# Two decode layers of cached attention and a gated feed-forward block: kept keys scored through PSUM in pairs of tiles, the last pairs' scores by unit, softmax sums inverted per head, the last column blocks in two PSUM tiles

## The chip, the cores and the metric

The kernel runs on one core of a Trainium2 chip. The metric is the device time of one execution in microseconds (us). Before the change the median of three runs is 1321.85 us (1321.67 to 1322.05).

## The reference

The reference runs two identical layers on two sequences (B = 2) with one new token each. All data are 32-bit floats. The weights and the caches are the same in both layers.

```python
B, Sq, D = 2, 1, 448
H, Sk, Dh = 16, 4096, 256          # feed-forward width F = 1792

def _A_ref(x, k_cache, v_cache, wq, wo):
    q = transpose((x @ wq).reshape(B, Sq, H, Dh), 0, 2, 1, 3)
    scores = einsum("bhqd,bhkd->bhqk", q, k_cache) * (Dh ** -0.5)
    p = softmax(scores)
    o = einsum("bhqk,bhkd->bhqd", p, v_cache)
    return transpose(o, 0, 2, 1, 3).reshape(B, Sq, H * Dh) @ wo

def _B_ref(x, W_gate, W_up, W_down):
    gate, up = x @ W_gate, x @ W_up
    return ((gate * (gate > 0)) * up) @ W_down

x = A_x
for _ in range(2):
    x = x + _A_ref(layernorm(x), A_k_cache, A_v_cache, A_wq, A_wo)
    x = x + _B_ref(layernorm(x), B_W_gate, B_W_up, B_W_down)
```

Keys and values of all heads and sequences are 268 MB, and each layer reads nearly all of them: the page counts 562.56 MB read.

## The kernel before

**Units and chunks.** A unit is one head of one sequence, so a layer has 32 units, numbered u in the order in which the layer treats them; the units 2j and 2j+1 are the two sequences of one head. The 4096 keys of a unit lie as 32 tiles of 128 partitions x 256 elements (`NT`), in four chunks (`NC`) of eight tiles (`CT`). A chunk is 1 MB, and so are the slots of `arena`, the one large SBUF buffer: 3 x 8 + 3 = 27 slots. The second layer treats the units in another order that begins with the last units of the first.

**Loads.** All loads are issued by SyncE (SP) from one list in a fixed order. `pump` issues the next loads while there are free slots, and `release` puts a slot back and pumps again. A load into a slot therefore waits for the last reader of the slot. 20 chunks (`KEPT`) at the end of the first layer stay in the arena for the second layer, and one value chunk more: the keys of the first layer's units 29, 30 and 31 (12 chunks) and the values of units 30 and 31, with one chunk of 29. The feed-forward weights follow: seven loads "in" (gate and up) and four loads "out". In the first layer the loads in0 to in4 find slots before the feed-forward block begins; in5 takes the slot of in0, which is free when TensorE has used in0, and what follows takes slots in the same way.

**Scores.** VectorE (DVE) multiplies a unit's keys with its query, and the products are summed over the 256 elements of a tile by VectorE or by ScalarE (ACT). Most units go through `score_block`: two products of 128x4096 in place (L378), eight tiles summed by ACT (L383), the rest by one reduction (L387). Units whose keys come in single chunks go through `score`:

- Kept keys must not be overwritten. Each tile is one scalar_tensor_tensor instruction (L419), which multiplies and sums at once; its product goes to `junk`, a part of the tile `down` that nobody reads. It has 8 such instructions per chunk.
- The last two units of the second layer (`CLOSING`) take four of a chunk's eight tiles by one product of 128x1024 (L410) and ACT (L412), the other four by L419 in place.
- Other chunks of the first units of the second layer share the eight tiles between L410 with ACT and L419 or L416 in other proportions.

**The loop over the units** is written out by hand in `attention`, and each engine keeps that order. Step u scores unit u chunk by chunk (c = 0 to 3), and between the chunks it finishes unit u-2: `out_add` (DVE, L475), `out_turn` (TensorE, L483), `out_keep` (DVE, L494), and `project` (TensorE, L504) if u-2 is odd. Then come `softmax_sum` of unit u-1 (L447) and the last chunk's scores; then the maximum (L428), the sum across the partitions by POOL, the exponentials (ACT, L438); then `weigh` of unit u-1, the product of its probabilities with its values (TensorE, L459), and `out_copy` of u-1 (ACT, L472). So TensorE does not weigh unit u-1 before `out_keep` of unit u-2, when that is odd, has run on VectorE in the middle of the scores of unit u.

**The division by the softmax sum** is in `out_turn`: the matmul that turns the row of results into a column is taken with `ri`, the inverted sum, as its moving operand.

**The feed-forward block** (`ffn`) multiplies with in0 to in6 (L569), turns the hidden values (L639), and multiplies with the four loads out0 to out3, one block of output columns each (`block`, L662). At the end of the kernel the four blocks go by turns into the two halves of one PSUM tile, `po_all`, and ACT copies each block out (L688). `busy` issues matmuls that nobody reads (L244).

Of the kernel before, what the change touches and what calls it, by code (L numbers as in the profile page):

```python
# [29 lines left out]
HASTE = 5  # L30
# [39 lines left out]
def two_layers(  # L70
# [9 lines left out]
    nc = tc.nc  # L80
# [58 lines left out]
    def get(*key):  # L139
        at = at_of[key]  # L140
        return arena[:, at * UNIT : (at + 1) * UNIT]

    def release(*key):
        units.free.add(at_of.pop(key))
        pump()
# [48 lines left out]

    row = consts.tile([P, 2 * DH], F32, name="row")
    down = consts.tile([P, D], F32, name="down")
    junk = down[:, :DH]
    y_end_row = row[SUMS : SUMS + B, D:]
    nc.scalar.dma_start(row[:B, :D], x.rearrange("b s d -> (b s) d"))
    pump()  # L200
# [4 lines left out]
    ones = consts.tile([P, 1], F32, name="ones")  # L205
# [26 lines left out]
    po_all = ps_o.tile([P, 2, 2 * DH], F32, name="po")  # L232
# [7 lines left out]
    def busy(n):  # L240


        unread = ps_q.tile([P, n * TAIL], F32, name="pq")
        nc.tensor.matmul(  # L244
            unread[:B], ident[:, :B], ident[:, None, :TAIL].to_broadcast([P, n, TAIL]),
            start=True, stop=True,
        )
# [46 lines left out]
    def attention(order, after, q_first=None, begun=None):  # L294
# [5 lines left out]
        q_of, oT_of, s_of, mx_of, p_of, r_of, po_of, pT_of = ({} for _ in range(8))  # L300
# [68 lines left out]
        def score_block(u, c):  # L369


            at = at_of["k", order[u], 0] * UNIT
            kt = arena[:, at : at + NC * UNIT].rearrange("p (t n) -> p t n", t=NT)
            if c == 0:
                s_of[u] = work.tile([P, NT], F32, name="scores")
            if c % 2 == 0:
                some = kt[:, c * CT : (c + 2) * CT, :]
                nc.vector.tensor_mul(  # L378
                    some, some, q_of[u][:, None, :].to_broadcast([P, 2 * CT, DH])
                )  # L380
            if c == 0:
                for t in range(CT):
                    nc.scalar.activation(  # L383
                        kt[:, t, :], kt[:, t, :], AF.Copy, accum_out=s_of[u][:, t : t + 1]
                    )
            if c == NC - 1:
                nc.vector.reduce_sum(s_of[u][:, CT:], kt[:, CT:, :], axis=AX.X)  # L387
                blocks.remove(("k", order[u]))
                for k in range(NC):
                    release("k", order[u], k)  # L390

        def score(u, c):
            kept = ("k", order[u], c) in after
            if ("k", order[u]) in blocks and not kept and not (ahead and u < HASTE):
                return score_block(u, c)
            kt = get("k", order[u], c).rearrange("p (t n) -> p t n", t=CT)
            if c == 0:
                s_of[u] = work.tile([P, NT], F32, name="scores")
            found = s_of[u][:, c * CT : (c + 1) * CT]
            by_act = 0 if kept else BY_ACT  # L400
            whole = CT
            if ahead and (u < HASTE or u >= n_u - CLOSING):
                by_act = CT // 2 if u > 0 else BY_ACT if c > 0 else 0
                whole = by_act
            whole = whole if by_act else 0
            if by_act:


                some = kt[:, :whole, :]
                nc.vector.tensor_mul(some, some, q_of[u][:, None, :].to_broadcast([P, whole, DH]))  # L410
                for t in range(by_act):
                    nc.scalar.activation(  # L412
                        kt[:, t, :], kt[:, t, :], AF.Copy, accum_out=found[:, t : t + 1]
                    )
            if whole > by_act:
                nc.vector.reduce_sum(found[:, by_act:], kt[:, by_act:, :], axis=AX.X)  # L416
            else:
                for t in range(whole, CT):
                    nc.vector.scalar_tensor_tensor(  # L419
                        junk if kept else kt[:, t, :], kt[:, t, :], 1.0, q_of[u],  # L420
                        op0=ALU.mult, op1=ALU.mult, accum_out=found[:, t : t + 1],
                    )
            if not kept:
                release("k", order[u], c)
# [7 lines left out]
        def softmax_exp(u):  # L432
            b = order[u][1]
            nm = work.tile([P, 1], F32, name="nm")
            nc.scalar.activation(nm, mx_of.pop(u), AF.Copy, scale=nsr[:, b : b + 1])  # L435
            p_of[u] = work.tile([P, NT], F32, name="probs")
            rs = work.tile([P, 1], F32, name="rs")
            nc.scalar.activation(  # L438
                p_of[u], s_of.pop(u), AF.Exp, bias=nm, scale=sr[:, b : b + 1], accum_out=rs
            )  # L440
            r_of[u] = work.tile([P, 1], F32, name="total")
            nc.gpsimd.partition_all_reduce(r_of[u], rs, P, RED.add)  # L442

        def softmax_sum(u):
            total = r_of[u]
            r_of[u] = work.tile([P, 1], F32, name="ri")
            nc.vector.reciprocal(r_of[u], total)  # L447

        def weigh(u, c):

# [27 lines left out]
            )  # L478

        def out_turn(u):  # L480
            pT_of[u] = ps_s.tile([P, 2], F32, name="small")
            for c in range(2):
                nc.tensor.matmul(  # L483
                    pT_of[u][:, c : c + 1], row[:, c * P : (c + 1) * P], r_of[u],
                    start=True, stop=True,
                )
            if u == n_u - 1:
                busy(2)

        def out_keep(u):  # L490
            h, b = order[u]
            if h not in oT_of:
                oT_of[h] = work.tile([P, 2, B], F32, name="oT")
            nc.vector.tensor_copy(oT_of[h][:, :, b], pT_of.pop(u))  # L494

        def project(u):
            h = order[u][0]
# [22 lines left out]
        for u in range(n_u + 2):  # L520
# [19 lines left out]
            if ahead and u == 0:  # L540
                query(ahead)
            if_pair(softmax_sum, u - 1)
            if mixed:
                if_pair(weigh, u - 1, 2)
# [8 lines left out]
    def ffn(last):  # L553
# [4 lines left out]
        total = squares()  # L558
        if not last:
            h, b = second[0]  # L560
# [107 lines left out]
        if last:  # L668


            square = work.tile([P, B], F32, name="square")
            nc.vector.tensor_mul(square, rstd, rstd)
            close = work.tile([P, CLOSE, B], F32, name="close")
            for i, st in enumerate(stat[-CLOSE:]):
                nc.vector.tensor_mul(
                    close[:, i, :], square, st.rearrange("p (b r) -> p b r", b=B)[:, :, 0]
                )
            y_end = ps_f.tile([P, TAIL], F32, name="pf")[SUMS : SUMS + B]
            nc.tensor.matmul(y_end, unit, y_end_row, start=True, stop=False)
            pds = [po_all[:, c % 2, :D] for c in range(FULL + 1)]  # L680

            def to_y(at, stop):
                nc.tensor.matmul(y[:, at], scaled, down[:, at], start=False, stop=stop)

            for c in range(FULL):
                at = block(pds[c], c, range(14))
                release("out", "", c)
                nc.scalar.activation(down[:, at], pds[c][:, at], AF.Copy)  # L688
                if c > 0:
                    to_y(before, False)  # L690
                before = at
            at = block(pds[FULL], FULL, range(14 - CLOSE))
            nc.scalar.activation(down[:, at], pds[FULL][:, at], AF.Copy)
            to_y(before, True)
            nc.vector.tensor_copy(left, y_left)
            nc.sync.dma_start(found[:, : FULL * P], left)
            w = get("out", "", FULL)
            for i in range(CLOSE):
                k = 14 - CLOSE + i
                w_k = w[:, k * TAIL : (k + 1) * TAIL]  # L700
# [24 lines left out]
        total = work.tile([P, 1], F32, name="sums")  # L725
# [39 lines left out]
    found = out.rearrange("b s d -> (b s) d")  # L765
# [62 lines left out]
```

## Time and profile before

| what | value |
|---|---|
| median of three runs | 1321.85 us |
| the profiled execution | 1322.23 us, of which its span is 1320.3 us |
| TensorE matmuls busy | 579.8 us (44%) |
| VectorE busy | 994.1 us (75%) |
| ScalarE busy | 330.1 us (25%) |
| GpSimd busy | 101.6 us (8%) |
| read from memory | 562.56 MB, 426 GB/s over the span |

The profiled execution took 1.93 us more than its span, and 0.38 us more than the median. In the profile, times are microseconds from the span's start. A row of the timeline has the start, the duration, the engine, the line, the operation, its output and inputs, and the count of instructions merged in the row; in brackets stands the idle time before it and what ended that. A row of a group has the count, the busy time, the mean duration in ns, and the idle time before them.

### The profile page before, as it was taken

What the parts mean: (1) busy time and instruction counts of PE and PEld (TensorE: products, weight loads), DVE (VectorE), ACT (ScalarE), POOL (GpSimd) and SP (SyncE); (2) the same over time, 40 slices, a digit from 0 to 9 for tenths busy, and PEclk for the clock granted to TensorE, in tenths of its full rate; (3) what the DMA queues carried; (4) which work ended last, traced back from release to release, by engine and by line L of the source; (5) the groups of instructions that cost most, each with busy time, mean ns of one, the idle gap of its engine ahead of it and who ended that gap; (6) DMA issues with size and microseconds to landing.
All of it is one profiled execution on the core that took longest, in us unless ns stands there. A gap on an engine that the chain in (4) does not pass through costs nothing.

```text
span 1320.3 us, 10001 instructions
## 1 busy us (share of the span) xinstructions
PE 579.8 (44%) x3276; PEld 193.0 (15%) x3276; DVE 994.1 (75%) x953; ACT 330.1 (25%) x1416; POOL 101.6 (8%) x192
## 2 busy tenths in 40 slices
PE   3333354333443334434585454352443424534358
PEld 2111111111111111111141111110111101111113
DVE  4878787787777877788729987688786887877971
ACT  2212222122221222221026522122122221222251
POOL 0000000000000000010001131000000000000110
PEclk9665666656666667667697767656766656666579
DMA  9999999999999999999999999999999999999998
GB/s 407 435 439 429 423 429 441 428 437 431 424 440 430 437 433 425 433 427 430 420 385 415 430 431 438 433 429 435 433 432 433 431 429 437 433 425 430 429 421 334
DMA packets 22671, 563.21 MB, mean 427 GB/s; under 512 B 2520, under 2 KB 2652, under 8 KB 9564
## 3 DMA queue, kind: packets, MB, share of 16 engines
q1 hardware_dynamic: 22612, 562.57, 99.4%
q8 instruction: 26, 0.43, 0.1%
q14 instruction: 25, 0.20, 0.0%
q10 hardware_dynamic: 8, 0.00, 0.0%
HBM read 562.56 MB, written 0.00 MB: 426 GB/s over the span
## 4 chain that ended last, share of the span: by engine, by line
DMA 62%; DVE 25%; PE 8%; issue 1%; ACT 1%; POOL 1%; SPq 0%; DVEq 0%; POOLq 0%; ACTq 0%
DMA arena<-in_vk_dram 61%; DVE arena L378 13%; DVE scores L387 7%; PE po L459 2%; DVE arena L410 2%; DVE arena L419 2%; PE pq L337 1%; DMA arena<-in_w_in_dram 1%; PE acc L504 1%; POOL top L430 1%; DVE down L419 1%; DVE row L475 1%; PE pf L569 1%; PE po L662 1%; ACT arena L412 1%
## 5 line engine op out<-in xcount | busy, mean ns | idle before, releaser
L378 DVE TENSOR_TENSOR arena<-arena 128x4096 f32<-128x4096 f32 x102 | 450.8, 4420 | 215.8 <-DMA arena<-in_vk_dram 215.8
L387 DVE TENSOR_REDUCE scores<-arena 128x24 f32<-128x6144 f32 x53 | 346.2, 6533 | 0.0
L459 PE MATMUL po<-arena,probs 128*2 128x512 f32 x2048 | 313.1, 760 | 21.2 <-DMA arena<-in_vk_dram 12.9
L483 PE MATMUL small<-ri,row 128*128 128x1 f32 x256 | 61.6, 344 | 574.1 <-DVE row L475 574.1
L383 ACT ACTIVATE arena<-arena 128x256 f32<-128x256 f32 x424 | 170.2, 403 | 330.7 <-DVE arena L378 330.7
L483 PEld LDWEIGHTS small<-ri,row 128*128 128x128 f32 x256 | 56.1, 306 | 635.0 <-DVE row L475 635.0
L435 ACT ACTIVATE nm<-top,nsr 128x1 f32<-128x1 f32 x64 | 18.8, 294 | 361.5 <-POOL top L430 361.5
L504 PE MATMUL acc<-arena,oT 128*2 128x448 f32 x128 | 50.9, 893 | 109.0 <-DVE oT L494 109.0
L430 POOL PARTITION_ALL_REDUCE top<-mx x64 | 44.5, 695 | 628.5 <-DVE mx L428 628.5
L459 PEld LDWEIGHTS po<-arena,probs 128*2 128x2 f32 x2048 | 53.8, 98 | 228.0 <-issue 216.9
L337 PE MATMUL pq<-arena,xs 128*33 128x256 f32 x174 | 76.1, 605 | 12.6 <-DMA arena<-in_w_head_dram 12.6
L383 ACT ACTIVATION_READ_ACCUMULATOR arena<-arena 128x1 f32 x424 | 79.4, 187 | 0.0
L353 POOL PARTITION_BROADCAST arena<-arena x58 | 27.7, 547 | 479.1 <-ACT arena L349 479.1
L349 ACT ACTIVATE arena<-pq 33x256 f32<-33x256 f32 x29 | 10.9, 377 | 174.0 <-PE pq L341 174.0
L475 DVE SCALAR_TENSOR_TENSOR row<-po,lead,row 128x256 f32<-128x256 f32 x64 | 30.6, 479 | 29.6 <-ACT row L472 29.3
L412 ACT ACTIVATE arena<-arena 128x256 f32<-128x256 f32 x117 | 47.1, 404 | 15.4 <-DVE arena L410 15.0
L472 ACT ACTIVATE row<-po,lead 128x256 f32<-128x256 f32 x64 | 29.6, 462 | 45.5 <-PE po L459 45.5
L337 PEld LDWEIGHTS pq<-arena,xs 128*33 128x33 f32 x174 | 25.4, 163 | 80.1 <-issue 66.1
L410 DVE TENSOR_TENSOR arena<-arena 128x1024 f32<-128x1024 f32 (+1 forms) x24 | 33.4, 1392 | 1.9 <-DMA arena<-in_vk_dram 1.9
L442 POOL PARTITION_ALL_REDUCE total<-rs x64 | 28.8, 450 | 61.7 <-ACT probs L438 60.6
L419 DVE SCALAR_TENSOR_TENSOR down<-arena,pq 128x256 f32<-128x256 f32 x64 | 26.9, 420 | 6.2 <-DMA arena<-in_vk_dram 4.2
L419 DVE SCALAR_TENSOR_TENSOR arena<-arena 128x256 f32<-128x256 f32 x80 | 29.1, 418 | 0.0
(142 smaller groups left out, 365.8 us busy)
## 6 DMA issues: line engine op xcount, KB each, us to landing
arena<-in_vk_dram SPq DMA_DIRECT2D x16, 4096.0 KB, 40.1
arena<-in_w_head_dram SPq DMA_DIRECT2D x31, 896.0 KB, 32.0
arena<-in_vk_dram SPq DMA_DIRECT2D x27, 1024.0 KB, 14.6
arena<-in_vk_dram SPq DMA_DIRECT2D x12, 2048.0 KB, 38.8
arena<-in_w_in_dram SPq DMA_DIRECT2D x14, 896.0 KB, 27.1
arena<-in_w_out_dram SPq DMA_DIRECT2D x5, 896.0 KB, 8.9
arena<-in_vk_dram SPq DMA_DIRECT2D x47, 44.3
arena<-in_w_out_dram SPq DMA_DIRECT2D x1, 512.0 KB, 16.4
```

The lines of the kernel that those rows point to most:

```text
L337: nc.tensor.matmul(q, xs[:, c, :], w[:, c * DH : (c + 1) * DH], start=(c == 0), stop=False)
L378: nc.vector.tensor_mul(some, some, q_of[u][:, None, :].to_broadcast([P, 2 * CT, DH]))
L383: nc.scalar.activation(kt[:, t, :], kt[:, t, :], AF.Copy, accum_out=s_of[u][:, t : t + 1])
L387: nc.vector.reduce_sum(s_of[u][:, CT:], kt[:, CT:, :], axis=AX.X)
L410: nc.vector.tensor_mul(some, some, q_of[u][:, None, :].to_broadcast([P, whole, DH]))
L412: nc.scalar.activation(kt[:, t, :], kt[:, t, :], AF.Copy, accum_out=found[:, t : t + 1])
L419: nc.vector.scalar_tensor_tensor(junk if kept else kt[:, t, :], kt[:, t, :], 1.0, q_of[u], op0=ALU.mult, op1=ALU.mult, accum_out=found[:, ...
L430: nc.gpsimd.partition_all_reduce(mx_of[u], mx, P, RED.max)
L459: nc.tensor.matmul(po_of[u][32 * t : 32 * t + 2, :], p_of[u][:, n : n + 2], vt[:, 2 * t * DH : (2 * t + 2) * DH], start=(c == 0), stop=(c ...
L475: nc.vector.scalar_tensor_tensor(row[:, :DH], po_of.pop(u)[:, DH:], lead[:, 1:2], row[:, :DH], op0=ALU.mult, op1=ALU.add,)
L483: nc.tensor.matmul(pT_of[u][:, c : c + 1], row[:, c * P : (c + 1) * P], r_of[u], start=True, stop=True,)
L504: nc.tensor.matmul(acc[at : at + B], oT_of[h][:, c, :], wo[:, c * D : (c + 1) * D], start=(n < 3), stop=(n >= n_u - 3),)
```

## The change

Four edits:

1. A kept chunk is scored in four steps of two tiles. Each step is a product of 128x512 into a PSUM tile (`pf`, pool `ps_f`, two buffers) and a reduction of it to 128x2. `junk` is gone.
2. The last two units of the second layer take all eight tiles by one product of 128x2048; ACT sums four of them as before, and one reduction on VectorE sums the other four.
3. The two softmax sums of a head stand in one tile and are inverted by one instruction after the second unit. `out_turn` multiplies with ones, and `out_keep` runs once per head and multiplies both units' columns with the inverted sums.
4. At the end of the kernel the four column blocks go by turns into `po_all` and into a second PSUM tile from `ps_f`.

```diff
-    junk = down[:, :DH]
@@ score
             whole = CT
             if ahead and (u < HASTE or u >= n_u - CLOSING):
                 by_act = CT // 2 if u > 0 else BY_ACT if c > 0 else 0
-                whole = by_act
+                whole = by_act if u < HASTE else CT
             whole = whole if by_act else 0
...
-            if whole > by_act:
+            if kept:
+                for t in range(0, CT, 2):
+                    some = ps_f.tile([P, 2, DH], F32, name="pf")
+                    nc.vector.tensor_mul(
+                        some, kt[:, t : t + 2, :], q_of[u][:, None, :].to_broadcast([P, 2, DH])
+                    )
+                    nc.vector.reduce_sum(found[:, t : t + 2], some, axis=AX.X)
+            elif whole > by_act:
                 nc.vector.reduce_sum(found[:, by_act:], kt[:, by_act:, :], axis=AX.X)
             else:
                 for t in range(whole, CT):
                     nc.vector.scalar_tensor_tensor(
-                        junk if kept else kt[:, t, :], kt[:, t, :], 1.0, q_of[u],
+                        kt[:, t, :], kt[:, t, :], 1.0, q_of[u],
@@ softmax_exp, softmax_sum
-            r_of[u] = work.tile([P, 1], F32, name="total")
-            nc.gpsimd.partition_all_reduce(r_of[u], rs, P, RED.add)
+            if u % 2 == 0:
+                r_of[u] = work.tile([P, B], F32, name="total")
+            total = r_of[u - u % 2]
+            nc.gpsimd.partition_all_reduce(total[:, b : b + 1], rs, P, RED.add)
...
-            r_of[u] = work.tile([P, 1], F32, name="ri")
-            nc.vector.reciprocal(r_of[u], total)
+            if u % 2 == 0:
+                return
+            total = r_of[u - 1]
+            r_of[u - 1] = work.tile([P, B], F32, name="ri")
+            nc.vector.reciprocal(r_of[u - 1], total)
@@ out_turn, out_keep
-                    pT_of[u][:, c : c + 1], row[:, c * P : (c + 1) * P], r_of[u],
+                    pT_of[u - u % 2][:, c, b : b + 1], row[:, c * P : (c + 1) * P], ones,
...
-            nc.vector.tensor_copy(oT_of[h][:, :, b], pT_of.pop(u))
+            share = r_of.pop(u - 1)[:, None, :].to_broadcast([P, 2, B])
+            nc.vector.tensor_mul(oT_of[h], pT_of.pop(u - 1), share)
@@ ffn
-            pds = [po_all[:, c % 2, :D] for c in range(FULL + 1)]
+            pds = [po_all[:, 0, :D], ps_f.tile([P, D], F32, name="pf")] * 2
```

On VectorE, the beginning of the scores of the first layer's unit 30, a kept unit, stood before as follows (`mx` is the maximum of unit 29, `pq` the PSUM tile with the query, `row` that of `out_add`):

```order
228 L428 TENSOR_REDUCE mx<-scores 128x1 [waits DVE_49]
229 L419 SCALAR_TENSOR_TENSOR down,scores<-arena,pq 128x256 [waits DMAHW1_49,PE_49]
230 L419 SCALAR_TENSOR_TENSOR down,scores<-arena,pq 128x256 [waits DVE_49] x7
231 L475 SCALAR_TENSOR_TENSOR row<-po,lead,row 128x256 [waits Activation_49]
232 L419 SCALAR_TENSOR_TENSOR down,scores<-arena,pq 128x256 [waits DVE_49] x16
233 L494 COPY oT<-small 128x2 [waits PE_49]
```

and it stands now as follows, up to the beginning of its second chunk:

```order
227 L434 TENSOR_REDUCE mx<-scores 128x1 [waits DVE_49]
228 L417 TENSOR_TENSOR pf<-arena,pq 128x512 [waits DMAHW1_49,PE_49]
229 L420 TENSOR_REDUCE scores<-pf 128x2 [waits DVE_49]
230 L417 TENSOR_TENSOR pf<-arena,pq 128x512
231 L420 TENSOR_REDUCE scores<-pf 128x2 [waits DVE_49]
232 L417 TENSOR_TENSOR pf<-arena,pq 128x512
233 L420 TENSOR_REDUCE scores<-pf 128x2 [waits DVE_49]
234 L417 TENSOR_TENSOR pf<-arena,pq 128x512
235 L420 TENSOR_REDUCE scores<-pf 128x2 [waits DVE_49]
236 L485 SCALAR_TENSOR_TENSOR row<-po,lead,row 128x256 [waits Activation_49]
237 L417 TENSOR_TENSOR pf<-arena,pq 128x512
```

A chunk has eight instructions as before, each of them over twice as many elements; the reduction waits for the product in front of it, where each scalar_tensor_tensor waited for the one in front of it because both wrote `down`.

On TensorE, the last column blocks stood before as follows (`po` is `po_all`, L683 adds a block to the result):

```order
587 L662 MATMUL po<-arena,row 32x128 [waits DMAHW1_49,Activation_49]
588 L662 MATMUL po<-arena,row 32x128 x13
589 L683 MATMUL acc<-down,scaled 2x128
590 L662 MATMUL po<-arena,row 32x128 [waits DMAHW2_49,Activation_49]
591 L662 MATMUL po<-arena,row 32x128 x7
592 L662 MATMUL po<-arena,row 32x128 [waits DMAHW3_49]
```

and the same rows stand now as:

```order
587 L676 MATMUL pf<-arena,row 32x128 [waits DMAHW1_49,PE_49]
588 L676 MATMUL pf<-arena,row 32x128 x13
589 L697 MATMUL acc<-down,scaled 2x128 [waits Activation_49]
590 L676 MATMUL po<-arena,row 32x128 [waits DMAHW2_49]
591 L676 MATMUL po<-arena,row 32x128 x7
592 L676 MATMUL po<-arena,row 32x128 [waits DMAHW3_49]
```

The wait for ACT's copy of the block before has moved from the first matmul of a block to the small matmul behind it.

More of the change, by code (lines that the diff above doesn't have):

```diff
@@ L440, in softmax_exp @@
             )
-            r_of[u] = work.tile([P, 1], F32, name="total")
-            nc.gpsimd.partition_all_reduce(r_of[u], rs, P, RED.add)
+            if u % 2 == 0:
+                r_of[u] = work.tile([P, B], F32, name="total")
+            total = r_of[u - u % 2]
+            nc.gpsimd.partition_all_reduce(total[:, b : b + 1], rs, P, RED.add)
         def softmax_sum(u):
-            total = r_of[u]
-            r_of[u] = work.tile([P, 1], F32, name="ri")
-            nc.vector.reciprocal(r_of[u], total)
+            if u % 2 == 0:
[3 more added lines that the diff above has]
+            nc.vector.reciprocal(r_of[u - 1], total)
         def weigh(u, c):
@@ L480, in out_turn @@
         def out_turn(u):
-            pT_of[u] = ps_s.tile([P, 2], F32, name="small")
+            b = order[u][1]
+            if u % 2 == 0:
+                pT_of[u] = ps_s.tile([P, 2, B], F32, name="small")
             for c in range(2):
                 nc.tensor.matmul(
-                    pT_of[u][:, c : c + 1], row[:, c * P : (c + 1) * P], r_of[u],
+                    pT_of[u - u % 2][:, c, b : b + 1], row[:, c * P : (c + 1) * P], ones,
                     start=True, stop=True,
@@ L490, in out_keep @@
         def out_keep(u):
[L491 to L494, printed above, removed]
+            if u % 2 == 0:
+                return
+            h = order[u][0]
+            oT_of[h] = work.tile([P, 2, B], F32, name="oT")
+            share = r_of.pop(u - 1)[:, None, :].to_broadcast([P, 2, B])
+            nc.vector.tensor_mul(oT_of[h], pT_of.pop(u - 1), share)
         def project(u):
```

## Prediction

> **What bounds the kernel now.** I read the page's slices and the chain first: the DMA engines are busy in every slice, and the chain that ends last is mostly loads.
>
> ```profile
> DMA  9999999999999999999999999999999999999998
> DMA 62%; DVE 25%; PE 8%; issue 1%; ACT 1%; POOL 1%; SPq 0%; DVEq 0%; POOLq 0%; ACTq 0%
> ```
>
> So a slower engine costs time only where it makes the loads stand still, or behind the last load. The view by stretches shows one place where they do:
>
> ```profile
> 300.00:600.00 300.00, 122.18 (x650) 37.99 (x641) 234.88 (x104) 69.53 (x304) 21.44 (x43) 0.65 1.00 432
> 668.00:673.00 5.00, 4.71 (x48) 2.30 (x47) 1.65 (x10) 1.71 (x3) 0.00 (x0) 1.00 0.54 201
> 671.00:672.00 1.00, 1.00 (x16) 0.37 (x12) 0.00 (x0) 0.00 (x0) 0.00 (x0) 1.00 0.19 79
> 673.00:680.00 7.00, 7.00 (x54) 2.73 (x46) 0.66 (x4) 1.17 (x3) 0.00 (x0) 1.00 1.01 414
> ```
>
> The last two numbers are the DMA share and GB/s. From 668 to 673 us, between the layers, the share is 0.54: 5 x 0.46 = 2.3 us lost in the mean over the engines; at its lowest, 0.19, some three of 16 engines still work. The arena is full of kept chunks and the next load, in5, waits for the slot of in0. The timeline gives the chain into that place:
>
> ```profile
> 604.08 0.42 DVE L419 SCALAR_TENSOR_TENSOR down<-arena 128x256 f32<-128x256 f32 x1
> ...
> 619.28 0.19 DVE L428 TENSOR_REDUCE mx<-scores 128x1 f32<-128x32 f32 x1
> 623.69 0.42 DVE L419 SCALAR_TENSOR_TENSOR down<-arena,pq 128x256 f32<-128x256 f32 x1 [4.22 <-DMA arena<-in_vk_dram]
> ...
> 650.15 0.15 DVE L494 COPY oT<-small 128x2 f32<-128x2 f32 x1
> ...
> 653.98 0.19 DVE L428 TENSOR_REDUCE mx<-scores 128x1 f32<-128x32 f32 x1
> ```
>
> ```profile
> 650.36 0.91 PE L504 MATMUL acc<-arena,oT 128*2 128x448 f32 x2 [6.34 <-DVE oT L494]
> 655.05 0.41 ACT L438 ACTIVATE probs<-scores,nm,sr 128x32 f32<-128x32 f32 x1
> 657.65 0.47 ACT L472 ACTIVATE row<-po,lead 128x256 f32<-128x256 f32 x1 [2.10 <-PE po L459]
> 658.69 0.61 PE L483 MATMUL small<-ri,row 128*128 128x1 f32 x4 [0.42 <-DVE row L475]
> 663.82 0.11 PEld L459 LDWEIGHTS po<-arena,probs 128*2 128x2 f32 x8 [1.07 <-DMA arena<-in_vk_dram]
> 670.15 3.33 PE L569 MATMUL pf<-arena,xs 128*32 128x448 f32 x32
> 671.16 1.08 SPq L130 DMA_DIRECT2D arena<-in_w_in_dram  x2
> ```
>
> VectorE scores the kept units 29, 30 and 31 from 604.08 to 653.98 us, and has only one pause there, the 4.22 us. At 650.15 `out_keep` of unit 29 lets TensorE go on: it projects, weighs unit 30 and by 657.65 has set ACT free, and then weighs unit 31, whose last values land at 663.8. The feed-forward block starts at 670.15, and in5 is issued at 671.16. Kept scores and DMA meet here, and VectorE has 4.2 us of room.
>
> **Kept scores, removed and added.** Of the 32 instructions of unit 29, the ninth and the 24th, with nothing else between them, give (615.08 - 608.09) / 15 = 0.466 us for one:
>
> ```profile
> 608.09 0.41 DVE L419 SCALAR_TENSOR_TENSOR down<-arena 128x256 f32<-128x256 f32 x1
> 615.08 0.42 DVE L419 SCALAR_TENSOR_TENSOR down<-arena 128x256 f32<-128x256 f32 x1
> ```
>
> Two tiles cost 0.93. No row writes a product to PSUM or reduces one from there, so I take the same operations in the arena:
>
> ```profile
> L387 DVE TENSOR_REDUCE scores<-arena 128x24 f32<-128x6144 f32 x53 | 346.2, 6533 | 0.0
> L410 DVE TENSOR_TENSOR arena<-arena 128x1024 f32<-128x1024 f32 x20 | 24.3, 1214 | 1.9 <-DMA arena<-in_vk_dram 1.9
> L410 DVE TENSOR_TENSOR arena<-arena 128x2048 f32<-128x2048 f32 x4 | 9.1, 2279 | 0.0
> L416 DVE TENSOR_REDUCE scores<-arena 128x5 f32<-128x1280 f32 x4 | 5.9, 1486 | 0.1
> ```
>
> ```profile
> 748.00 2.28 DVE L410 TENSOR_TENSOR arena<-arena 128x2048 f32<-128x2048 f32 x1
> 750.31 1.49 DVE L416 TENSOR_REDUCE scores<-arena 128x5 f32<-128x1280 f32 x1
> 751.75 0.48 DVE L475 SCALAR_TENSOR_TENSOR row<-po,lead,row 128x256 f32<-128x256 f32 x1
> ```
>
> Products: (2279 - 1214) / 1024 = 1.04 ns per element, so 512 take 1214 - 512 x 1.04 = 0.68 us. Reductions: (6533 - 1486) / 4864 = 1.038 ns, so 512 take 0.69. A reduction that needs the product before it begins 0.03 us after its end (748.00 + 2.28 to 750.31); an instruction that needs nothing begins some 0.07 early (751.75 against 751.80). A step of two tiles is 0.68 + 0.03 + 0.62 = 1.33 us, 0.40 more than before: eight instructions a chunk as before, but two passes over the data.
>
> The bounds. For PSUM operands:
>
> ```profile
> L419 DVE SCALAR_TENSOR_TENSOR arena<-arena 128x256 f32<-128x256 f32 x80 | 29.1, 418 | 0.0
> L475 DVE SCALAR_TENSOR_TENSOR row<-po,lead,row 128x256 f32<-128x256 f32 x64 | 30.6, 479 | 29.6 <-ACT row L472 29.3
> L631 DVE TENSOR_TENSOR row<-pf,row 128x448 f32<-128x448 f32 x2 | 1.2, 624 | 9.0 <-PE pf L569 9.0
> ```
>
> L475, with `po` in PSUM, is 61 ns above L419: on both instructions at most 0.12, a step of 1.45. L631, a product with a PSUM input, is 624 against 1214 - 576 x 1.04 = 615, 9 ns more: nearer in kind, so I keep 1.33. If the reduction started as early as one that needs nothing, the step would be 0.13 shorter, 1.20. A gain is excluded as long as an element costs 1.04 ns in each pass: 2 x 512 x 1.04 = 1.06, above 0.93.
>
> The Trainium skill (Perfetto Trace Analysis, Optimizing Scalar/DVE Operations) gives VectorE about 60 ns of overhead per instruction on SBUF and about 125 on PSUM, which speaks against this edit; by it, 65 ns on the reduction make a step 1.39 and the end some 3 us later, while L631 shows 9 ns.
>
> **What it moves.** A unit of 16 steps is 21.28; `out_add` (0.48), a small instruction (L494, 0.15, shown below) and the maximum (0.19), each less 0.07 of overlap, add 0.6: 21.9 us. Unit 30 then starts at 604.08 + 21.9 = 626.0, the pause gone; unit 31 at 647.9; `out_keep` of unit 29, after 12 steps and `out_add`, at 647.9 + 16.0 + 0.4 = 664.2, against 650.15: 14.0 us later (rounded). Behind it wait `project`, the weighing of units 30 and 31, and the feed-forward block. The maximum of unit 31 comes at 669.6 and its exponentials end 1.5 later (653.98 to 655.46), at 671.0, just ahead of ACT's `out_copy` of unit 30 (657.65 + 14.0 = 671.7): TensorE's chain decides. The values of unit 31 have long landed, but TensorE hardly waits for them now (the 1.07 is the weight load's; its matmuls were filled up by `busy`). So the feed-forward block and in5 come 14.0 us later. The loads up to in4 find their slots in time: in4 needs the slot freed by that same `project`, some 2 us behind `out_keep`, at 666, before the share falls at 668.
>
> The loads then stand still: everything after in5 is saturated before (share 1.0 again from 673), so what is lost is not made up. Engines that were late had no idle time before and catch up now: between 0 and 2.3 us come back. I take 1: **13.0 us** at the end. `out_keep` has 16 + 16 + 12 = 44 steps ahead of it. At 1.20 per step it moves 44 x 0.13 = 5.7 us less, 8.3 (unit 30 then starts at 623.9, still just behind its keys); at 1.45 it moves 44 x 0.12 = 5.3 more, 19.3.
>
> **Sums inverted per head.** It removes 32 inversions and 32 copies; the copies are (the inversions have the same mean):
>
> ```profile
> L494 DVE COPY oT<-small 128x2 f32<-128x2 f32 x64 | 9.7, 152 | 2.8 <-PE small L483 2.8
> ```
>
> That is at most 64 x 0.152 = 9.7 us of VectorE in the whole kernel, nearly all of it ahead of pauses for loads like the 4.22 above: nothing at the end. `out_turn` no longer waits for the inversion, which came first anyway.
>
> **The last pairs.** A chunk was 1.15 (L410, 1269.41 to 1270.56) + 4 x 0.34 (L419) = 2.5 us on VectorE; by the rows above it becomes 2.31 + 1.14 = 3.4, and ACT's sums begin 1.1 later:
>
> ```profile
> 1269.41 1.23 DVE L410 TENSOR_TENSOR arena<-arena 128x1024 f32<-128x1024 f32 x1 [1.88 <-DMA arena<-in_vk_dram]
> 1270.56 0.42 DVE L419 SCALAR_TENSOR_TENSOR arena<-arena 128x256 f32<-128x256 f32 x1
> 1270.90 0.42 DVE L419 SCALAR_TENSOR_TENSOR arena<-arena 128x256 f32<-128x256 f32 x1
> 1284.11 1.90 PE L459 MATMUL po<-arena,probs 128*2 128x512 f32 x16 [1.76 <-DMA arena<-in_vk_dram]
> 1289.10 1.90 PE L459 MATMUL po<-arena,probs 128*2 128x512 f32 x16 [0.85 <-DMA arena<-in_vk_dram]
> 1293.97 1.04 PE L459 MATMUL po<-arena,probs 128*2 128x512 f32 x8 [0.59 <-DMA arena<-in_vk_dram]
> PE pf L569 <- DMA arena<-in_w_in_dram: 0.8, 2, 0.6
> ```
>
> Unit 30 ends 4 x 0.9 + 0.2 = 3.8 later, of which the 1.88 swallows half; three chunks of unit 31 add 2.7, so `out_keep` of unit 29 is 4.6 later. TensorE's waits for loads take 1.76 + 0.85 + 0.59 + 0.8 = 4.0 of it: 0.6 us is left.
>
> **The last blocks.** They drop three waits:
>
> ```profile
> PE po L662 <- ACT down L688: 1.1, 3, 0.4
> ```
>
> 1.1 us if nothing else is late. The 0.6 above uses half of it, and the last weight pieces still land while the blocks run:
>
> ```profile
> 1314.00:1315.00 1.00, 0.76 (x26) 0.48 (x18) 0.00 (x0) 0.22 (x1) 0.00 (x0) 1.00 0.32 121
> ```
>
> So I put both edits together at 0, between -0.5 and +1.
>
> **The rivals.**
>
> 1. *The dependence costs nothing* (step 1.20): 8.3 - 1 = +7.3, 1329 us. The Trainium skill (VectorE: DVE Perf Modes, The DRAIN you can't avoid) says that the next VectorE instruction cannot start before the pipe is empty, and that a semaphore between two costs nothing extra. Against it stand the 0.466 of dependent L419 rows beside 0.34 of independent ones (1270.56 to 1270.90), and the 0.03 above. Chance 0.10.
> 2. *Not slower*: PSUM passes at half the time per element make a step 0.80, below 0.93. Then VectorE is ahead, but the values of unit 31 still land at 663.8, so the middle gains nothing, and the end gains 0 to 1.1: 1321.3 us. It decides below a step of about 1.08, where the shift of `out_keep` is under 5 us. For it speaks only that no row shows these forms; against it that every 32-bit product and reduction in the trace takes 1.04 ns an element. Chance 0.08.
> 3. *PSUM costs much more*, a step of 1.6 by write and read: 44 x 0.27 = 12 more, 1347 us. Chance 0.07.
>
> **How the numbers follow.** My forecast, steps between 1.25 and 1.45, has 0.75: span 1320.3 + 13.0 = 1333.3, execution 1333.3 + 1.93 = 1335.2, and 0.38 less on the scale of the median: 1334.9 us. The range goes from rival 1 with the whole 2.3 back (1321.9 + 6.0 = 1327.9, taken as 1327) to 1321.9 + 19.3 + 1 = 1342. A measurement of this kernel tells 0.2% (2.6 us) from no change: rival 2 is split, faster 0.03 and same 0.05; same gets 0.01 from the forecast's low end, 0.06; slower has 0.91.
>
> **What would show it.** Right: L417 to L417 about 1.33 us apart; no pause before unit 30; the first L569 between the layers near 684; a DMA share near zero for some 10 us before 685; the rest of the second layer shifted as a whole. Wrong: a step under 1.1, in5 issued before 676, or a time lost in the last 60 us.

## The result, and the profile after

The changed kernel takes 1337.08 us, the median of four runs (1336.19 to 1337.58), against 1321.84 us of the kernel before beside it (1321.67 to 1322.05): a ratio of 1.0113, with a 95% interval from 1.0101 to 1.0126. It is 15.2 us slower. The profiled execution of it took 1336.77 us, with a span of 1335.0 us, 14.7 us more than before.

The page of the changed kernel, its slices of the DMA engines and the chain that ends last:

```profile
DMA  9999999999999999999959999999999999999998
DMA 62%; DVE 27%; PE 7%; issue 1%; ACT 1%; POOL 1%; SPq 0%; DVEq 0%; POOLq 0%; ACTq 0%
```

One slice has fallen from 9 to 5, and VectorE has two points more of the chain. The view by stretches of the changed kernel tells where that is (the third number of the busy times is VectorE; the last three are the granted TensorE clock, the DMA share and GB/s):

```profile
600.00:660.00 60.00, 17.94 (x104) 8.02 (x100) 57.88 (x90) 3.59 (x12) 2.59 (x6) 0.64 1.00 425
666.00:687.00 21.00, 19.50 (x138) 6.55 (x134) 7.39 (x22) 3.66 (x8) 0.73 (x2) 0.95 0.25 86
673.00:686.00 13.00, 12.16 (x87) 4.68 (x90) 2.63 (x14) 2.39 (x4) 0.00 (x0) 1.00 0.01 3
```

VectorE is busy for 57.88 of these 60 us, which from 604 on are scores of the kept units. Then the loads stand still: for 13 us the DMA share is 0.01, and over the 21 us around them 21 x 0.75 = 15.8 us are lost, where 2.3 were lost between 668 and 673 us before. Over one and the same stretch, 655 to 690 us, the share falls from 0.94 to 0.54, which is 35 x 0.40 = 14.0 us. So the added loss of loading time in this one place, 13.5 to 14 us, is nearly the whole 14.7.

The groups of the kept scores on VectorE, with different shapes apart (count, busy time, mean ns of one, idle time before them):

```profile
L420 DVE TENSOR_REDUCE scores<-pf 128x2 f32<-128x512 f32 x48 | 33.2, 692 | 1.7
L417 DVE TENSOR_TENSOR pf<-arena,pq 128x512 f32<-128x512 f32 x32 | 22.0, 687 | 0.6 <-PE pq L315 0.6
L417 DVE TENSOR_TENSOR pf<-arena 128x512 f32<-128x512 f32 x16 | 11.1, 692 | 0.0
```

The timeline of the changed kernel has the same stretch in order of time. L434 is the maximum of a unit (units 29, 30 and 31 in turn), L508 at 665.00 is `out_keep` of the head of units 28 and 29, L518 is `project`, L482 is `out_copy`, L583 is the feed-forward block's first product, and the last row is the issue of in5:

```profile
604.05 0.69 DVE L417 TENSOR_TENSOR pf<-arena 128x512 f32<-128x512 f32 x1
604.78 0.69 DVE L420 TENSOR_REDUCE scores<-pf 128x2 f32<-128x512 f32 x1
605.38 0.69 DVE L417 TENSOR_TENSOR pf<-arena 128x512 f32<-128x512 f32 x1
...
620.44 0.15 DVE L508 TENSOR_TENSOR oT<-small,ri 128x4 f32<-128x4 f32 x1
620.65 1.66 PE L518 MATMUL acc<-arena,oT 128*2 128x448 f32 x4 [9.72 <-DVE oT L508]
622.24 2.25 PE L307 MATMUL pq<-arena,xs 128*128 128x256 f32 x6
...
625.96 0.19 DVE L434 TENSOR_REDUCE mx<-scores 128x1 f32<-128x32 f32 x1
626.72 0.70 DVE L417 TENSOR_TENSOR pf<-arena,pq 128x512 f32<-128x512 f32 x1 [0.57 <-PE pq L315]
...
665.00 0.15 DVE L508 TENSOR_TENSOR oT<-small,ri 128x4 f32<-128x4 f32 x1
665.21 0.91 PE L518 MATMUL acc<-arena,oT 128*2 128x448 f32 x2 [9.69 <-DVE oT L508]
...
670.51 0.19 DVE L434 TENSOR_REDUCE mx<-scores 128x1 f32<-128x32 f32 x1
...
672.29 0.47 ACT L482 ACTIVATE row<-po,lead 128x256 f32<-128x256 f32 x1 [0.21 <-PE po L469]
684.50 3.21 PE L583 MATMUL pf<-arena,xs 128*32 128x448 f32 x32
685.51 1.41 SPq L130 DMA_DIRECT2D arena<-in_w_in_dram  x2
```

A step is 605.38 - 604.05 = 1.33 us. The 4.22 us pause for the keys of unit 30 is gone, and 0.57 us of another stand in its place. `out_keep` comes at 665.00 instead of 650.15 (14.85 later), the feed-forward block at 684.50 instead of 670.15 (14.35), and in5 is issued at 685.51 instead of 671.16 (14.35).

### The profile page after: what moved, and what is told of

Same layout as the page of the kernel before. It is cut to its first block, busy times and chain, and to the rows that moved or that the text cites. A ratio compares the mean times of both kernels' runs of the same rounds, so it can differ in the third digit from the quotient of the medians.

```text
span 1335.0 us, 9779 instructions
## 1 busy us (share of the span) xinstructions
PE 563.1 (42%) x3276; PEld 191.3 (14%) x3276; DVE 1022.1 (77%) x737; ACT 328.9 (25%) x1416; POOL 104.5 (8%) x192
## 4 chain that ended last, share of the span: by engine, by line
DMA 62%; DVE 27%; PE 7%; issue 1%; ACT 1%; POOL 1%; SPq 0%; DVEq 0%; POOLq 0%; ACTq 0%
DMA arena<-in_vk_dram 58%; DVE arena L377 12%; DVE scores L386 7%; DMA arena<-in_w_in_dram 2%; DVE scores L420 2%; PE po L469 2%; DVE pf L417 2%; DVE arena L409 2%; PE pq L336 1%; DMA arena<-in_w_out_dram 1%; PE acc L518 1%; DVE arena L425 1%; DVE row L485 1%; DMA arena<-in_w_head_dram 1%; POOL top L436 1%
## 5 line engine op out<-in xcount | busy, mean ns | idle before, releaser
L495 PE MATMUL small<-ones,row 128*128 128x1 f32 x256 | 62.8, 349 | 607.0 <-DVE row L485 607.0
L495 PEld LDWEIGHTS small<-ones,row 128*128 128x128 f32 x256 | 57.3, 312 | 668.4 <-DVE row L485 668.4
L518 PE MATMUL acc<-arena,oT 128*2 128x448 f32 x128 | 50.9, 893 | 117.2 <-DVE oT L508 117.2
L436 POOL PARTITION_ALL_REDUCE top<-mx x64 | 47.7, 745 | 660.2 <-DVE mx L434 660.2
L336 PE MATMUL pq<-arena,xs 128*33 128x256 f32 x174 | 71.8, 576 | 14.1 <-DMA arena<-in_w_head_dram 14.1
L409 DVE TENSOR_TENSOR arena<-arena 128x1024 f32<-128x1024 f32 (+1 forms) x24 | 42.0, 1749 | 0.0
L482 ACT ACTIVATE row<-po,lead 128x256 f32<-128x256 f32 x64 | 29.4, 459 | 22.7 <-PE po L469 22.5
L420 DVE TENSOR_REDUCE scores<-pf 128x2 f32<-128x512 f32 x48 | 33.2, 692 | 1.7
L444 ACT ACTIVATE probs<-scores,nm,sr 128x32 f32<-128x32 f32 x64 | 26.4, 413 | 2.1
## 6 DMA issues: line engine op xcount, KB each, us to landing
arena<-in_w_out_dram SPq DMA_DIRECT2D x1, 512.0 KB, 16.5
```

What stands on the lines that cost most here:

```text
L336: nc.tensor.matmul(q, xs[:, c, :], w[:, c * DH : (c + 1) * DH], start=(c == 0), stop=False)
L420: nc.vector.reduce_sum(found[:, t : t + 2], some, axis=AX.X)
L436: nc.gpsimd.partition_all_reduce(mx_of[u], mx, P, RED.max)
L495: nc.tensor.matmul(pT_of[u - u % 2][:, c, b : b + 1], row[:, c * P : (c + 1) * P], ones, start=True, stop=True,)
L518: nc.tensor.matmul(acc[at : at + B], oT_of[h][:, c, :], wo[:, c * D : (c + 1) * D], start=(n < 3), stop=(n >= n_u - 3),)
```

## The experiments

Theory A is the chain of the prediction: the load queue sets the end, VectorE's time counts only as far as it makes `out_keep` of unit 29 late, and through it the feed-forward block and in5. (That the loads wait for in5's slot is read from the traces; no run gave in5 another slot.) Its rivals put the loss into the other edits, or let VectorE's work count one for one wherever it is added or taken (theory C). The table has all runs, each against the kernel before measured beside it; a start is that of the first row named, from one execution's timeline of each kernel.

| kernel | median us (runs) | ratio, 95% interval | `out_keep` of 29 at | feed-forward at |
|---|---|---|---|---|
| before, as profiled | 1321.84 (4) | | 650.15 | 670.15 |
| after | 1337.08 (4) | 1.0101 to 1.0126 | 665.00 | 684.50 |
| e1_scores_only | 1338.52 (4) | 1.0105 to 1.0135 | 665.71 | 685.26 |
| e2_without_scores | 1321.99 (10) | 0.9989 to 1.0007 | 649.99 | 669.53 |
| e3_unit29_only | 1325.69 (9) | 1.0018 to 1.0038 | 653.78 | 672.60 |
| e4_unit31_only | 1326.73 (5) | 1.0022 to 1.0048 | 655.17 | 674.73 |
| e5_pairs_only | 1322.16 (11) | 0.9991 to 1.0009 | 650.24 | 670.17 |
| e6_blocks_only | 1321.78 (11) | 0.9989 to 1.0006 | 649.71 | 669.38 |
| e7_sums_only | 1322.21 (11) | 0.9993 to 1.0011 | 649.94 | 669.83 |
| e8_two_junks | 1322.02 (11) | 0.9991 to 1.0008 | 646.65 | 669.83 |
| e9_sums_by_act | 1324.68 (10) | 1.0008 to 1.0027 | 653.46 | 673.20 |
| e10_best | 1321.93 (11) | 0.9990 to 1.0008 | 646.60 | 669.72 |

The kernel before had medians of 1322.08 us beside e1 to e4, 1322.15 beside e5, e6, e8 and e9, and 1322.07 beside e7 and e10.

**The kept scores alone, and all but them.** e1 is the kernel before with this edit only; e2 is the changed kernel with kept tiles scored as before:

```diff
+            if kept:
+                for t in range(0, CT, 2):
+                    some = ps_f.tile([P, 2, DH], F32, name="pf")
+                    nc.vector.tensor_mul(
+                        some, kt[:, t : t + 2, :], q_of[u][:, None, :].to_broadcast([P, 2, DH])
+                    )
+                    nc.vector.reduce_sum(found[:, t : t + 2], some, axis=AX.X)
```

> The kernel before with edit 1 alone (kept scores through PSUM). Theory A (a kept step of two tiles costs VectorE 1.33 us instead of 0.93, the feed-forward block between the layers comes later by it, and the loads stand still for as long): the whole loss, 1336 to 1337 us, the first L569 between the layers at 684 to 685. Rival B (the loss is shared with the edits at the end of the kernel): 1334 us or less.

> The changed kernel with edit 1 undone (kept scores by scalar_tensor_tensor again; edits 2, 3 and 4 stay). Theory A: 1321.3 to 1322.3 us, no measurable difference from before. Rival B: 1324 us or more.

The kept scores alone cost 16.4 us, the other three edits together nothing that the runs can tell. So the whole loss is edit 1, as theory A has it. e1's median is even 1.4 us above that of the changed kernel. Its timeline and one stretch of it, then the same stretch of the changed kernel, show where half of that comes from in the two profiled executions:

```profile
622.15 2.93 PE L308 MATMUL pq<-arena,xs 128*128 128x256 f32 x6
627.36 0.69 DVE L418 TENSOR_TENSOR pf<-arena,pq 128x512 f32<-128x512 f32 x1 [1.24 <-PE pq L316]
...
685.26 3.21 PE L576 MATMUL pf<-arena,xs 128*32 128x448 f32 x32
```

```profile
622.00:625.00 3.00, 3.00 (x9) 2.32 (x8) 2.93 (x5) 0.00 (x0) 0.00 (x0) 0.50 0.94 404
```

```profile
622.00:625.00 3.00, 3.00 (x14) 2.39 (x13) 2.93 (x5) 0.00 (x0) 0.00 (x0) 0.72 0.94 404
```

The same products for the query take 2.93 us in e1 and 2.25 in the changed kernel, and the granted TensorE clock over this stretch is 0.50 there and 0.72 here; so VectorE waits 1.24 us for the query of unit 30 instead of 0.57, and the feed-forward block is 0.76 later.

**Only one of the three kept units.** In e3 the condition above is `kept and u == 29`, in e4 `kept and u == 31`; everything else is as before. Under theory A the room of 4.2 us ahead of unit 30 swallows most of what unit 29 adds, and none of what unit 31 adds ahead of `out_keep` (12 steps); under theory C a unit counts in full.

> The kernel before with edit 1 in unit 29 alone, the first kept unit. VectorE works 6.4 us longer there. Theory A: the pause of 4.2 us ahead of unit 30 takes most of it, so out_keep of unit 29 and the end come 2 to 2.6 us later, 1324 us, and the pause ahead of unit 30 is gone. Rival C (the loss goes with the work added, a third of 15 us for each unit, wherever it stands): 1327 us.

> The kernel before with edit 1 in unit 31 alone, the last kept unit. The same 6.4 us of added work, but with no pause behind it; 12 of its 16 steps stand ahead of out_keep of unit 29 (12 x 0.40 = 4.8 us), the rest beside TensorE's weighing of unit 30. Theory A: 4.5 to 5.2 us later, 1326.7 us. Rival C: 1327 us, as with unit 29. A and C differ in the difference of these two runs: 2.5 us by A, none by C.

The timeline of e3, then of e4:

```profile
626.83 0.42 DVE L426 SCALAR_TENSOR_TENSOR down<-arena,pq 128x256 f32<-128x256 f32 x1 [0.59 <-PE pq L316]
...
653.78 0.15 DVE L501 COPY oT<-small 128x2 f32<-128x2 f32 x1
672.60 3.21 PE L576 MATMUL pf<-arena,xs 128*32 128x448 f32 x32
```

```profile
623.42 0.42 DVE L426 SCALAR_TENSOR_TENSOR down<-arena,pq 128x256 f32<-128x256 f32 x1 [4.12 <-DMA arena<-in_vk_dram]
...
655.17 0.15 DVE L501 COPY oT<-small 128x2 f32<-128x2 f32 x1
674.73 3.21 PE L576 MATMUL pf<-arena,xs 128*32 128x448 f32 x32
```

e4 came as theory A expected: the pause ahead of unit 30 is as long as before, 4.12 us, and the 12 slow steps of unit 31 make `out_keep` 5.0 us later. e3 gave more than expected: unit 30 starts 3.1 us late, of which 0.6 is the wait for the query, which the expectation had left out, and `out_add` then waits 0.41 for ScalarE; `out_keep` is 3.6 us later, the feed-forward block 2.45, the median 3.6. By the medians alone the two differ by 1.0 us with overlapping intervals, which does not separate the theories: a third of the whole loss, 5 us for each, would fit e4 as well. The traces speak for theory A, with the pause swallowed in e3 and whole in e4; what excludes theory C is e8, below.

**The other edits, one at a time.** e5 has only `whole = by_act if u < HASTE else CT`, e7 only the inversion once a head, e6 only this:

```diff
-            pds = [po_all[:, c % 2, :D] for c in range(FULL + 1)]
+            pds = [po_all[:, 0, :D], ps_f.tile([P, D], F32, name="pf")] * 2
```

> The kernel before with edit 2 alone (the last two units' products by 128x2048). VectorE works 7 us longer for the last two units, ahead of out_keep of unit 29. Theory A: TensorE's waits for loads behind it (4.0 us in all in the profile before) take all but some 0.3 to 0.6 us: 1322.2 to 1322.8 us, with the first L569 of the last feed-forward block 1 to 1.7 us later against the loads. Rival E (nothing hides it): 1325 us or more.

> The kernel before with edit 4 alone (the last column blocks in two PSUM tiles). The three waits for ScalarE's copies, 1.1 us, go. Theory A: the last weight pieces land while the blocks run and hold the blocks instead, so 0.1 to 0.4 us are gained at most: 1321.6 to 1322.1 us. Rival F (the waits were the bound): 1.1 us gained, 1320.9 us.

> The kernel before with the sums inverted once a head alone. Theory A: no difference that can be measured, 1321.6 to 1322.5; each product of out_keep and its like stays at 0.15 us, the feed-forward starts at 669.5 to 670.2. Theory C: up to 1 us faster, since 64 inversions of some 0.06 us leave VectorE.

None of them makes a difference that can be measured. In e5's timeline the last feed-forward block starts 1.27 us later than before (1300.30), and one wait for a load is still left in it:

```profile
1301.57 3.21 PE L569 MATMUL pf<-arena,xs 128*32 128x448 f32 x32
...
1309.63 0.96 PE L569 MATMUL pf<-arena,xs 128*32 128x448 f32 x8 [0.34 <-DMA arena<-in_w_in_dram]
```

In e6's timeline the three waits for ACT (1.1 us) are gone, and three waits for loads stand in their places, 0.44 + 0.30 + 0.17 = 0.91 us:

```profile
1313.42 0.96 PE L662 MATMUL pf<-arena,row 128*32 128x128 f32 x26 [0.44 <-DMA arena<-in_w_out_dram]
...
1315.51 0.52 PE L662 MATMUL po<-arena,row 128*32 128x128 f32 x10 [0.30 <-DMA arena<-in_w_out_dram]
...
1316.32 0.47 PE L662 MATMUL pf<-arena,row 128*32 128x64 f32 x18 [0.17 <-DMA arena<-in_w_out_dram]
```

In e7 the inversions and copies fall from 128 instructions with 9.7 + 9.7 us to 64 with 9.9 us by its groups, and the end stays. The 64 x 0.06 us of the expectation are 3.8 us, not up to 1; by theory C they would have shown.

```profile
L451 DVE RECIPROCAL ri<-total 128x2 f32<-128x2 f32 x32 | 5.0, 156 | 0.0
L502 DVE TENSOR_TENSOR oT<-small,ri 128x4 f32<-128x4 f32 x32 | 4.9, 154 | 1.4 <-PE small L489 1.4
```

**A faster VectorE.** If a slower VectorE loses time in this place, does a faster one win some? In e8, the kernel before with two scratch tiles by turns, no product of a kept tile goes to the tile that the one ahead of it writes:

```diff
-    junk = down[:, :DH]
+    junks = [down[:, :DH], row[:, DH:]]
...
-                        junk if kept else kt[:, t, :], kt[:, t, :], 1.0, q_of[u],
+                        junks[t % 2] if kept else kt[:, t, :], kt[:, t, :], 1.0, q_of[u],
```

> The kernel before, with the products of kept tiles written by turns to two pieces nobody reads instead of one, so that an instruction no longer waits for the one in front: 0.34 us a tile instead of 0.466, 11.7 us less for VectorE in the three kept units. Theory A: out_keep of unit 29 comes 5 to 6 us sooner, but the last values of unit 31 land at 663.8 us as before and hold the feed-forward block, so the time is that of before, 1321.6 to 1322.4 us. Rival C (time goes with VectorE's work in the kept units in both directions): 1313 us.

```profile
604.04 0.41 DVE L419 SCALAR_TENSOR_TENSOR down<-arena 128x256 f32<-128x256 f32 x1
604.38 0.42 DVE L419 SCALAR_TENSOR_TENSOR row<-arena 128x256 f32<-128x256 f32 x1
604.73 0.42 DVE L419 SCALAR_TENSOR_TENSOR down<-arena 128x256 f32<-128x256 f32 x1
...
623.52 0.42 DVE L419 SCALAR_TENSOR_TENSOR down<-arena,pq 128x256 f32<-128x256 f32 x1 [7.59 <-DMA arena<-in_vk_dram]
...
638.05 0.42 DVE L419 SCALAR_TENSOR_TENSOR down<-arena,pq 128x256 f32<-128x256 f32 x1 [2.78 <-DMA arena<-in_vk_dram]
...
646.65 0.16 DVE L494 COPY oT<-small 128x2 f32<-128x2 f32 x1
653.64 3.20 PE L459 MATMUL po<-arena,probs 128*2 128x512 f32 x16 [1.96 <-DMA arena<-in_vk_dram]
...
669.83 3.41 PE L569 MATMUL pf<-arena,xs 128*32 128x448 f32 x32
```

In this timeline of e8 the instructions are 0.345 us apart instead of 0.466, a quarter less. What it wins goes to the pauses: 7.59 us instead of 4.22 ahead of unit 30, 2.78 ahead of unit 31, where there was none, and 1.96 us on TensorE for the values. `out_keep` is 3.5 us earlier and not the expected 5 to 6, because of the new pause for the keys of unit 31. The feed-forward block is 0.3 earlier, the median not measurably. Theory C would have had some 9 us; it falls.

**The product to PSUM without the second pass.** e9 writes the same products to `pf`, and ACT sums them, a tile at a time:

```diff
+                    for i in range(2):
+                        nc.scalar.activation(
+                            some[:, i, :], some[:, i, :], AF.Copy,
+                            accum_out=found[:, t + i : t + i + 1],
+                        )
```

> The kernel before with kept products through PSUM as in edit 1, but summed by ScalarE, tile by tile, in place of the reduction on VectorE: one pass on VectorE, 0.6 us for two tiles, and 0.8 us on ScalarE beside it. Theory A (VectorE's second pass is the loss): a step of 0.80 to 0.85 us, the feed-forward block between the layers starts at 670 as before, 1321.6 to 1322.6 us. Rival D (products through PSUM are slow as such, or the extra instructions on ScalarE push its chain back): 1325 us or more.

```profile
612.44 0.70 DVE L418 TENSOR_TENSOR pf<-arena 128x512 f32<-128x512 f32 x1 [0.19 <-ACT pf L422]
613.34 0.70 DVE L418 TENSOR_TENSOR pf<-arena 128x512 f32<-128x512 f32 x1 [0.19 <-ACT pf L422]
...
628.46 0.69 DVE L418 TENSOR_TENSOR pf<-arena,pq 128x512 f32<-128x512 f32 x1 [2.98 <-ACT pf L422]
...
673.20 3.21 PE L580 MATMUL pf<-arena,xs 128*32 128x448 f32 x32
```

The expectation of no difference was missed: 2.5 us slower. In the timeline of e9 the product is as long as in the changed kernel, and a step is 613.34 - 612.44 = 0.90 us, a little less than the 0.93 of before: without the second pass VectorE does not fall behind here. But ACT, which sets that pace, keeps its order as well: where a unit begins, the exponentials and `out_copy` stand ahead of the sums, `out_copy` waits for TensorE's weighing (5.01 us at 627.06), and VectorE waits for the sums (2.98 us ahead of one row). This is the second half of rival D. `out_keep` is 3.3 us late, the feed-forward block 3.05, and the end follows them again.

**A version to beat both.** e10 is the kernel before with the two scratch tiles of e8 and edits 3 and 4.

> The kernel before with the products of its kept tiles by turns in two scratch tiles and with the sums' inversion once a head and the two tiles for the last blocks; the kept scores and the last pairs stay as before. Theory A (the load queue sets the end, VectorE only when it is late for the feed-forward): 1321.5 to 1322.1, that is between 0.6 us faster and no difference, with the feed-forward starting at 669.5 to 670.2 and a DMA loss of 1 to 2.5 us ahead of it. Theory C (VectorE's time counts one for one): 1312 to 1314.

It is not measurably faster. By its view of stretches the loads are a little busier between the layers, 0.72 instead of 0.54, which is 5 x 0.18 = 0.9 us:

```profile
668.00:673.00 5.00, 4.86 (x47) 2.39 (x48) 1.64 (x10) 1.28 (x1) 0.00 (x0) 1.00 0.72 241
```

The profiled span is 1319.8 us, 0.5 less than before; the medians differ by 0.14 us. So of the kernels tried none beats the one before.

## Why the prediction was right, point by point

**The step of two tiles** was put at 0.68 + 0.03 + 0.62 = 1.33 us and is 1.33: the reduction starts 0.73 after the product (0.69 + 0.04), the next product 0.60 after that. The estimate from the arena's rows held for PSUM: 687 to 692 ns against 0.68, and 692 ns against 0.69. The ends of its range did not show: neither 61 ns more for PSUM, nor the 65 ns by which the two figures of the Trainium skill differ (Perfetto Trace Analysis, Optimizing Scalar/DVE Operations), is in the 692 ns of the reduction, and rival 3 with 1.6 falls.

**Rival 1**, that a dependence costs nothing, falls by two pairs of rows: the reduction begins 0.04 us after the end of the product that it needs, the next product 0.09 before the end of the reduction; and the same instruction is 0.345 from the next one in e8 and 0.466 where both write one tile. The Trainium skill's sentence that a semaphore costs nothing extra (VectorE: DVE Perf Modes, The DRAIN you can't avoid), which rests there on copies, does not carry over to these rows: with the dependence each instruction here takes 0.12 us more. The 0.345 agrees with another sentence of that section, that a next instruction which is not held starts earlier. Rival 2 needed a step under 1.08.

**The room ahead of unit 30** is used up as predicted, but what is late next was missed. Unit 30 was to start at 626.0 and starts at 626.72: it waits 0.57 us for its query. TensorE makes that query behind `project` of the head before, and `project` behind `out_keep` at 620.44, which on VectorE stands behind 12 slow steps of unit 29. The prediction followed this chain for unit 29's head and not for the one ahead of it. Hence `out_keep` at 665.00 instead of 664.2. Two smaller readings: the exponentials of unit 31 end just ahead of `out_copy` of unit 30, as the prediction has it (ACT waits 0.21 us there for TensorE), and in4 was issued at 666.96, a little late and not in time (over 666 to 668 us the DMA share is 0.78, before 0.98); the stretch ends with in5 all the same.

**The feed-forward block** moved by 14.35, and 14.0 was predicted. That it came so close is in part luck, for two misses cancel here: `out_keep` is 0.85 later than said, and 0.5 us of the chain between the two is gone (20.00 us before, 19.50 after). The prediction had TensorE hardly waiting for the last values. From `out_copy` of unit 30 to that of unit 31 it takes 7.28 us before (657.65 to 664.93) and 6.98 after (672.29 to 679.27), and 6.98 in e1, e4 and e9 too, where the values had landed: so the wait for them was 0.3 us. The other 0.2 lie ahead of `out_copy` of unit 30, where the granted clock stays at 0.50 from 650 to 655 us before and from 665 to 668 after; that the clock makes them is not shown.

**What comes back** is the term that came out wrong: 1 us was taken off, between 0 and 2.3, because late DMA engines would catch up. The span grew by 14.7, 0.35 more than in5 moved. In the profiled runs of the other four kernels that move the feed-forward block it is the same side: the span grew by 16.5, 2.9, 5.9 and 3.2 us (e1, e3, e4, e9) where the block moved by 15.11, 2.45, 4.58 and 3.05, that is 0.15 to 1.4 more. These are single executions: e4's is the slowest of its five, and e9's median is only 2.5 us above that of the kernel before. So what the runs show is that next to nothing came back. Nor do the loads behind it run faster, by the stretch of the second layer of the kernel before and then of the changed one:

```profile
690.00:1290.00 600.00, 259.78 (x1362) 80.27 (x1365) 474.22 (x474) 175.90 (x775) 59.71 (x94) 0.65 1.00 430
```

```profile
690.00:1290.00 600.00, 259.62 (x1473) 85.06 (x1465) 471.52 (x383) 169.14 (x750) 61.47 (x92) 0.64 1.00 430
```

What makes the extra 0.15 to 1.4 us stays open, and it is no more than one execution differs from another by. The large reductions of `score_block` in the second layer lie 13.9 to 15.1 us later in the changed kernel than in the one before, up and down along the layer; in e2 and e10, whose medians are those of the kernel before, they lie 0.04 to 1.3 us earlier. And 0.5 GB/s of 430, the rounding of this column, is already 0.7 us in 600.

**Sums inverted per head** were put at nothing, and e7 shows nothing. **The last pairs and the last blocks** were put at 0 together, and e2 shows 0 for the three edits. The rows agree with the working in the main: in e5 `out_keep` of the second layer's unit 29 is 5.4 us later (1282.81 instead of 1277.37) where 4.6 was put; in the changed kernel the last feed-forward block starts at 1316.93, 1.9 us later than the 14.7 of everything else, there is no wait for loads left in it, and the blocks have short waits for loads in place of the three for ACT, by its view of waits from 1295 us on:

```profile
PE po L676 <- DMA arena<-in_w_out_dram: 0.3, 1, 0.3
PE pf L676 <- DMA arena<-in_w_out_dram: 0.2, 1, 0.2
```

**The sum**: 1334.9 was predicted and 1337.08 measured. Of the 2.2 us, 1.7 are in the span: 0.35 by the feed-forward block and 1.35 by the loads that do not catch up. The rest is the scale: the profiled execution was 0.38 above the median before and is 0.31 below it after, less 0.16 of time outside the span.

## What to carry to other kernels

Count passes over the data before instructions: one fused product and sum of 256 elements, even at 0.466 us with its dependence, is cheaper than half of a 1.33 us pair of passes over 512. In a kernel that its loads bound, look for the places where the loads stand still, and follow the chain into each with every handover of every engine in it, the one a unit earlier too; here time on VectorE was free up to the room there and counted nearly one for one beyond it, and a gain on it gave nothing. Of the loading time lost in front of the saturated queue, next to none was made up in these runs; count it in full.

## What the runs showed of the hardware

- VectorE writes a 32-bit product of 512 elements to PSUM in 687 to 692 ns and reduces it from there in 692; the arena's rows give 0.68 and 0.69 us. No surcharge for PSUM shows in these forms.
- Two scalar_tensor_tensor instructions in a row that write one scratch tile are 0.466 us apart, with two tiles by turns 0.345, although nobody reads the product.
- After a wait TensorE's granted clock is low for some us, and not always for equally long. Ahead of the query of unit 30 it had waited for `out_keep` in three kernels: 6.39 us in the kernel before, 9.72 in the changed kernel and 9.72 in e1. The six products of 128x256 then took 2.24 us in the kernel before, 2.25 in the changed kernel and 2.93 in e1, at a granted clock of 0.73, 0.72 and 0.50 over the three us from 617 (before) and 622 us on. So VectorE waits for the query in the changed kernel because the query begins 5 us later, not because of the clock; only in e1 does the clock add to it. Why it rose later there the runs do not show. The row and the stretch of the kernel before:

```profile
617.23 2.24 PE L308 MATMUL pq<-arena,xs 128*128 128x256 f32 x6
617.00:620.00 3.00, 3.00 (x14) 2.41 (x13) 2.29 (x11) 0.00 (x0) 0.35 (x1) 0.73 0.99 426
```
